# A linear-attention and GEGLU kernel: x transposed by DMA at the start, K, Q and G in 512+128 columns, a padded down projection and a bf16 Z row

## The chip, the cores and the metric

One core of a Trainium2 chip runs the whole program. The metric is the device time of one execution in microseconds (us). Nearly all executions agree within 0.3%; an execution over 1.5% above the fastest is called slow and is left out of the verdicts (in this study one of the kernel before's runs, 294.08 us, was slow; every other timed run is fast, and a kernel run only once has the state unknown). The profile is a separate recording of one execution. Its span is about 1.7 us shorter than the time of the same execution (282.7 against 284.45 before).

## The reference

```python
x = A_x                                        # 1 x 2048 x 640, bf16
g = sigmoid((x * gate_w).sum(-1, keepdims=True))
a = linear_attention(x)                        # 32 heads of 20, phi(t) = (t>0 ? t+1 : exp(t)) + 1e-6
b = (gelu(x @ w_gate) * (x @ w_up)) @ w_down   # inner width 1728
return g * a + (1 - g) * b
```

In the attention, kv = sum over s of phi(k) v, z = sum over s of phi(k), and o = phi(q) kv / (phi(q) z), then o @ wo.

## The kernel before

The kernel keeps one stream of matmuls on TensorE and hides the rest behind it. Its stages, in order:

- the head: weights and x arrive, x is transposed into xT;
- E(0): gate and up projection of the first 512 rows, in column tiles ft = 0 to 13;
- K: phi(x wk); then Q and G together, where G = x^T phi(k) replaces V;
- E(1), with the small products KV (wv^T G) and M (kv wo) in between;
- F: the output rows, 128 at a time. F(0) to F(3), E(2), F(4) to F(7), E(3), F(8) to F(15).

D(t) is a VectorE chain, which normalises row tile t of phi(q). F(t) needs it. ps tiles are the eight PSUM accumulators.

The head, on SP's queue and on TensorE:

```python
NWARM = 7                                      # dummy 128x512 matmuls on zeros
dma(out=x_sb[0][:, 0:2, :], in_=x_view[:, 0:2, :])
dma(out=wg[:, :, 0:256], in_=wg_v[:, :, 0:256])
dma(out=wu[:, :, 0:256], in_=wu_v[:, :, 0:256])
dma(out=x_sb[0][:, 2:4, :], in_=x_view[:, 2:4, :])
# ... cut ...
transpose_x(0); transpose_x(1)                 # 5 PE transposes each, copied out by ACT and DVE
# ft = 0 and 1 in halves of 256 rows: gate, gate, up, up; then transpose_x(2), (3), and again
```

The down projection. The inner width 1728 is 13.5 times 128, so the last product has only 64 rows. The two column halves hh put it in different rows of the array, next to each other:

```python
for hh in range(2):
    lo = hh * FL                               # FL = 64
    nc.tensor.matmul(accs[hh][:, 0:HALF], lhsT=hT[lo : lo + FL, NF - 1, ts],
                     rhs=wd[lo : lo + FL, NF - 1, css[hh]], start=True, stop=False)
for hh in range(2):
    # 5 matmuls with pqT and M, then 13 with hT and wd, 320 columns each; eviction: hh 0 ACT, hh 1 DVE
```

The Z row, replicated over the partitions by a product with ones in fp32:

```python
nc.tensor.matmul(zp[:, 0:HALF], lhsT=ones_f[:], rhs=zacc[:, cs], start=True, stop=True)
```

Of the kernel before, what the change touches and what calls it, by code (L numbers as in the profile page):

```python
# [16 lines left out]
def kernel(  # L17
# [21 lines left out]
    NQ = 4  # L39
# [7 lines left out]
    NWARM = 7  # L47
# [35 lines left out]
    ident = consts.tile([P, P], BF16, name="ident")  # L83
    make_identity(nc, ident[:])
    zeros_bf = consts.tile([P, QW], BF16, name="zeros_bf")
    nc.vector.memset(zeros_bf[:], 0.0)
    ones_f = consts.tile([P, P], FP32, name="ones_f")
    nc.gpsimd.memset(ones_f[:], 1.0)

    dma = nc.sync.dma_start  # L90
    dma(out=x_sb[0][:, 0:2, :], in_=x_view[:, 0:2, :])
    dma(out=wg[:, :, 0:256], in_=wg_v[:, :, 0:256])
    dma(out=wu[:, :, 0:256], in_=wu_v[:, :, 0:256])
    dma(out=x_sb[0][:, 2:4, :], in_=x_view[:, 2:4, :])
# [13 lines left out]
    for q in (1, 2, 3):  # L108
        dma(out=x_sb[q][:], in_=x_view[:, 4 * q : 4 * q + 4, :])
# [5 lines left out]
    dma(out=wd[FL:P, NF - 1, :], in_=B_w_down[FM:F, :])  # L115
# [17 lines left out]

    eneg = consts.tile([P, NT], FP32, name="eneg")
    gsc = {}

    def transpose_x(st):
        q, sl = divmod(st, 4)
        tp = psum.tile([P, 2 * QW], BF16, name="tp_x", tag="ps")
        for dk in range(ND):  # L140
            nc.tensor.transpose(
                tp[:, dk * P : (dk + 1) * P], x_sb[q][:, sl, dk * P : (dk + 1) * P], ident[:]
            )
        nc.scalar.copy(  # L144
            out=xT[q][:, 0:2, sl * P : (sl + 1) * P],
            in_=tp[:, 0 : 2 * P].rearrange("p (k n) -> p k n", k=2),
        )
        nc.vector.tensor_copy(
            out=xT[q][:, 2:5, sl * P : (sl + 1) * P],
            in_=tp[:, 2 * P : 5 * P].rearrange("p (k n) -> p k n", k=3),  # L150
        )

    hT_cur = {}
    hT0 = big.tile([P, NF, QW], BF16, name="hT0")
    hT_cur[0] = hT0
# [11 lines left out]
    def phase_E(q, ft):  # L167
# [6 lines left out]
        else:  # L174
# [4 lines left out]
            for lo in (0, FL):  # L179
                nc.vector.tensor_tensor(out=hT_cur[q][lo : lo + FL, ft, :], in0=pgu[FL:P, :],  # L180
                                        in1=gl[0:FL, :], op=ALU.mult)

    def phi(dst, src, width):
        e = work.tile([P, HALF], BF16, name="phi_e")
        nc.scalar.activation(out=e[:, :width], in_=src, func=ACT.Exp)  # L185
        m = work.tile([P, HALF], BF16, name="phi_m")
# [14 lines left out]

    def phase_K(st):
        ps0 = ps_tile("ps_k")
        proj(ps0, st, 0, HALF)
        phi(pk[st][:, 0:HALF], ps0[:, 0:HALF], HALF)
        ps1 = ps_tile("ps_k")
        proj(ps1, st, HALF, D + 1)
        phi(pk[st][:, HALF:D], ps1[:, 0:HALF], HALF)
        nc.scalar.activation(
            out=eneg[:, st : st + 1], in_=ps1[:, HALF : HALF + 1], func=ACT.Exp, scale=-1.0  # L210
        )

    def phase_Q(st, hh):
        ps = ps_tile("ps_q")
        proj(ps, st, D + 1 + hh * HALF, D + 1 + (hh + 1) * HALF)
        phi(pq[st][:, hh * HALF : (hh + 1) * HALF], ps[:, 0:HALF], HALF)

    g_sb = big.tile([P, ND, D], BF16, name="g_sb")
    g_ps = {}

    def phase_G(st, hh):
        q, sl = divmod(st, 4)
        for ct in range(ND):
            if st == 0:
                g_ps[hh, ct] = ps_tile("ps_G")
            nc.tensor.matmul(  # L226
                g_ps[hh, ct][:, 0:HALF], lhsT=x_sb[q][:, sl, ct * P : (ct + 1) * P],
                rhs=pk[st][:, hh * HALF : (hh + 1) * HALF], start=(st == 0), stop=(st == NT - 1),
            )

    def g_out(hh):
        for ct in range(ND):
            dst = g_sb[:, ct, hh * HALF : (hh + 1) * HALF]
# [8 lines left out]
    def phase_Z(st):  # L242
        if st == 0:
            return
        nc.vector.tensor_tensor(out=zacc[:], in0=(pk[0][:] if st == 1 else zacc[:]), in1=pk[st][:], op=ALU.add)
# [210 lines left out]
```

## Time and profile before

| | before |
|---|---|
| time, median of the first 5 runs | 283.5 us |
| time, median of the 15 runs up to the result | 283.94 us (283.21 to 284.61) |
| span of the profile | 282.7 us |
| TensorE busy | 97% of the span |

From the page of the kernel before: the line of busy times (engine, us, share of the span, number of instructions), and the two lines of the chain that ended last, by engine and by source line.

```profile
PE 275.6 (97%) x1708; PEld 164.2 (58%) x1721; DVE 146.1 (52%) x323; ACT 80.8 (29%) x172; POOL 2.8 (1%) x10
...
PE 95%; DMA 2%; issue 0%; SPq 0%; ACT 0%; DVE 0%; DVEq 0%
PE ps_acc L356 20%; PE ps_u L159 20%; PE ps_g L159 19%; PE ps_acc L353 8%; PE ps_q L197 8%; PE ps_k L197 8%; PE ps_G L226 8%; DMA wu<-in_B_w_up_dram 2%; PE ps_gu L159 2%; PE ps_acc L348 1%; PE ps_m L303 1%; PE ps_kv L274 1%; PE ps_z L251 0%; ACT xT L144 0%; DVE o_out L362 0%
```

TensorE is the chain from its first real work to its last. VectorE, busy for half of the span, is nearly absent from the chain. So a change gains what it takes out of the TensorE stream, plus what it takes from the two ends.

In the timeline each row has a start, a duration, an engine, a source line, the instruction with its shape and a count; the bracket is the idle time just before it and what ended it. Durations of matmuls overlap, so the cost of a group is the start of the next group minus its own start. The head of the kernel before, TensorE only:

```profile
4.75 0.74 PE L141 MATMUL tp_x<-ident,x_all 128*128 128x128 bf16 x5
5.95 1.43 PE L159 MATMUL ps_g<-xT,wg 128*128 128x256 bf16 x10 [0.46 <-ACT xT L144]
8.06 1.26 PE L159 MATMUL ps_u<-xT,wu 128*128 128x256 bf16 x10 [0.68 <-DMA wu<-in_B_w_up_dram]
9.16 0.72 PE L141 MATMUL tp_x<-ident,x_all 128*128 128x128 bf16 x10
10.34 1.25 PE L159 MATMUL ps_g<-xT,wg 128*128 128x256 bf16 x10 [0.46 <-ACT xT L144]
11.43 1.26 PE L159 MATMUL ps_u<-xT,wu 128*128 128x256 bf16 x10
12.52 0.81 PE L159 MATMUL ps_g<-xT,wg 128*128 128x512 bf16 x2
```

The last line is ft=2, where the halves of 256 rows end. Ten dense matmuls of 256 columns take 1.09 us (10.34 to 11.43); the first ten took 2.11 (5.95 to 8.06), as wu had not landed.

One row tile of F begins like this (start of F(1), timeline of TensorE):

```profile
141.80 0.57 PE L356 MATMUL ps_acc<-wd,hT 128*128 128x320 bf16 x3
142.30 0.31 PE L348 MATMUL ps_acc<-wd,hT 64*128 64x320 bf16 x2
142.54 0.85 PE L353 MATMUL ps_acc<-m_all,pqT 128*128 128x320 bf16 x5
```

Three full matmuls at the spacing of 136 ns should end 0.41 us after 141.80, but the 64-row pair starts after 0.50. The pair itself takes 0.24.

The Z product and the M block (timeline of TensorE; four passes for two fp32 products, and twelve products for M):

```profile
85.21 1.24 PE L251 MATMUL ps_z<-zacc,ones_f 128*128 128x320 f32 x4
86.29 0.84 PE L226 MATMUL ps_G<-pk,x_all 128*128 128x320 bf16 x5
...
109.99 2.21 PE L303 MATMUL ps_m<-wo_g,kvt 120*120 120x320 bf16 x12
112.14 1.04 PE L159 MATMUL ps_g<-xT,wg 128*128 128x512 bf16 x3
```

The end of the span (timeline, all engines): one eviction of 320 columns, one store.

```profile
279.32 0.55 DVE L362 TENSOR_SCALAR o_out<-ps_acc,omg_all 128x320 bf16<-128x320 f32 x1 [4.69 <-PE ps_acc L356]
279.94 0.33 SPq L365 DMA_DIRECT2D out_dram<-o_out  x1
```

### The profile page before, as it was taken

How to read it: one execution, taken by the hardware profiler on the slowest of the kernel's cores; microseconds unless marked ns; L12 is line 12 of the kernel's file. 1: busy time of each engine (PE TensorE's matmuls, PEld its weight loads, DVE VectorE, ACT ScalarE, POOL GpSimd, SP SyncE). 2: the span in 40 equal slices, each digit the busy share in tenths (PEclk: the TensorE clock that was granted, in tenths of full speed). 3: DMA queues.
4: the chain of work that ended last, by engine and by line, in shares of the span. 5: the costliest groups of instructions: out<-in, count | busy, mean ns of one | idle time of the engine just before them, and what ended most of it. 6: DMA issues, size and time to landing. Idle time of an engine off the chain costs nothing.

```text
span 282.7 us, 4315 instructions
## 1 busy us (share of the span) xinstructions
PE 275.6 (97%) x1708; PEld 164.2 (58%) x1721; DVE 146.1 (52%) x323; ACT 80.8 (29%) x172; POOL 2.8 (1%) x10
## 2 busy tenths in 40 slices
PE   7899999999999999999999999999999999999995
PEld 4644467767777765444566544456654445666663
DVE  1223369999978999999992132231113333010010
ACT  3222277753353345232200222320022222101000
POOL 3000000000000000000000000000000000000000
PEclk9999999999999999999999999999999999999999
DMA  7999999400000221332233000000100000001001
GB/s 205 330 305 186 260 361 272 150 2 0 2 1 0 49 46 27 103 83 46 50 70 96 23 0 0 2 0 23 49 23 0 2 0 0 26 23 46 26 30 40
DMA packets 35441, 20.91 MB, mean 74 GB/s; under 512 B 21214, under 2 KB 35422, under 8 KB 35422
## 3 DMA queue, kind: packets, MB, share of 16 engines
q1 hardware_dynamic: 35422, 20.65, 27.4%
q8 instruction: 13, 0.21, 0.3%
q14 instruction: 6, 0.05, 0.1%
HBM read 12.62 MB, written 2.62 MB: 54 GB/s over the span
## 4 chain that ended last, share of the span: by engine, by line
PE 95%; DMA 2%; issue 0%; SPq 0%; ACT 0%; DVE 0%; DVEq 0%
PE ps_acc L356 20%; PE ps_u L159 20%; PE ps_g L159 19%; PE ps_acc L353 8%; PE ps_q L197 8%; PE ps_k L197 8%; PE ps_G L226 8%; DMA wu<-in_B_w_up_dram 2%; PE ps_gu L159 2%; PE ps_acc L348 1%; PE ps_m L303 1%; PE ps_kv L274 1%; PE ps_z L251 0%; ACT xT L144 0%; DVE o_out L362 0%
## 5 line engine op out<-in xcount | busy, mean ns | idle before, releaser
L159 PE MATMUL ps_g<-xT,wg 128*128 128x512 bf16 (+1 forms) x257 | 64.1, 371 | 1.6 <-ACT xT L144 0.9
L159 PE MATMUL ps_u<-xT,wu 128*128 128x512 bf16 (+1 forms) x270 | 64.6, 371 | 0.7 <-DMA wu<-in_B_w_up_dram 0.7
L165 DVE TENSOR_TENSOR hT<-ps_u,gl 128x512 bf16<-128x512 f32 x52 | 35.6, 686 | 56.5 <-PE ps_u L159 56.5
L356 PE MATMUL ps_acc<-wd,hT 128*128 128x320 bf16 x416 | 61.7, 299 | 0.0
L164 ACT ACTIVATE gl<-ps_g 128x512 bf16<-128x512 f32 x52 | 30.9, 597 | 79.9 <-PE ps_g L159 76.8
L356 PEld LDWEIGHTS <-hT 128*128 128x128 bf16 x416 | 40.7, 98 | 15.8
L159 PEld LDWEIGHTS <-wu 128*128 128x128 bf16 x270 | 26.3, 98 | 30.7 <-DMA wu<-in_B_w_up_dram 1.0
L159 PEld LDWEIGHTS <-wg 128*128 128x128 bf16 x270 | 26.2, 98 | 30.2 <-issue 1.7
L362 DVE TENSOR_SCALAR o_out<-ps_acc,omg_all 128x320 bf16<-128x320 f32 x16 | 8.8, 550 | 61.6 <-PE ps_acc L356 61.6
L197 PEld LDWEIGHTS <-xT 128*128 128x128 bf16 x320 | 31.1, 97 | 12.8 <-issue 0.2
L359 ACT ACTIVATE o_out<-ps_acc,omg_all 128x320 bf16<-128x320 f32 x16 | 8.4, 527 | 68.0 <-PE ps_acc L356 68.0
L353 PE MATMUL ps_acc<-m_all,pqT 128*128 128x320 bf16 x160 | 27.1, 300 | 0.0
L197 PE MATMUL ps_q<-wqk,xT 128*128 128x320 bf16 x160 | 26.5, 299 | 0.0
L226 PE MATMUL ps_G<-pk,x_all 128*128 128x320 bf16 x160 | 26.4, 298 | 0.0
L197 PE MATMUL ps_k<-wqk,xT 128*128 128x320 bf16 (+1 forms) x160 | 22.0, 299 | 0.0
L185 ACT ACTIVATE phi_e<-ps_q 128x320 bf16<-128x320 f32 x32 | 14.0, 437 | 26.4 <-PE ps_q L197 22.7
L226 PEld LDWEIGHTS <-x_all 128*128 128x128 bf16 x160 | 15.5, 97 | 6.3 <-issue 0.2
L353 PEld LDWEIGHTS <-pqT 128*128 128x128 bf16 x160 | 14.3, 98 | 7.2
L190 DVE SCALAR_TENSOR_TENSOR pq<-ps_q,phi_m 128x320 bf16<-128x320 f32 x32 | 15.3, 480 | 0.3
L187 DVE TENSOR_SCALAR phi_m<-phi_e 128x320 bf16<-128x320 bf16 x64 | 13.8, 231 | 2.7 <-ACT phi_e L185 2.7
L185 ACT ACTIVATE phi_e<-ps_k 128x320 bf16<-128x320 f32 x32 | 13.7, 438 | 3.9 <-PE ps_k L197 3.6
L190 DVE SCALAR_TENSOR_TENSOR pk<-ps_k,phi_m 128x320 bf16<-128x320 f32 x32 | 14.4, 482 | 0.0
(52 smaller groups left out, 122.7 us busy)
## 6 DMA issues: line engine op xcount, KB each, us to landing
out_dram<-o_out SPq DMA_DIRECT2D x16, 160.0 KB, 1.8
wd<-in_B_w_down_dram SPq DMA_DIRECT2D x1, 2080.0 KB
x_all<-in_A_x_dram SPq DMA_DIRECT2D x3, 640.0 KB, 7.2
wqk<-in_A_wqkv_dram SPq DMA_DIRECT2D x2, 800.0 KB
wg<-in_B_w_gate_dram SPq DMA_DIRECT2D x1, 800.0 KB
wu<-in_B_w_up_dram SPq DMA_DIRECT2D x1, 800.0 KB
wv<-in_A_wqkv_dram SPq DMA_DIRECT2D x1, 800.0 KB
wo_g<-in_A_wo_dram SPq DMA_DIRECT2D x1, 750.0 KB, 14.7
```

What stands on the lines that cost most here:

```text
L159: nc.tensor.matmul(ps[:, t0 : t0 + tw], lhsT=w[:, dk, ft * P : (ft + 1) * P], rhs=xT[q][:, dk, t0 : t0 + tw], start=(dk == 0), stop=(dk == ...
L164: nc.scalar.activation(out=gl[:], in_=psg[:], func=ACT.Gelu_apprx_tanh)
L165: nc.vector.tensor_tensor(out=hT_cur[q][:, ft, :], in0=psu[:], in1=gl[:], op=ALU.mult)
L185: nc.scalar.activation(out=e[:, :width], in_=src, func=ACT.Exp)
L187: nc.vector.tensor_scalar(out=m[:, :width], in0=e[:, :width], scalar1=1.0, scalar2=EPS, op0=ALU.min, op1=ALU.add,)
L190: nc.vector.scalar_tensor_tensor(out=dst, in0=src, scalar=0.0, in1=m[:, :width], op0=ALU.max, op1=ALU.add,)
L197: nc.tensor.matmul(ps[:, 0 : hi - lo], lhsT=xT[q][:, dk, sl * P : (sl + 1) * P], rhs=wqk[:, dk, lo:hi], start=(dk == 0), stop=(dk == ND - 1),)
L226: nc.tensor.matmul(g_ps[hh, ct][:, 0:HALF], lhsT=x_sb[q][:, sl, ct * P : (ct + 1) * P], rhs=pk[st][:, hh * HALF : (hh + 1) * HALF], start= ...
L353: nc.tensor.matmul(acc[:, 0:HALF], lhsT=pqT[q][:, dk, ts], rhs=M["sb"][:, dk, cs], start=False, stop=False)
L356: nc.tensor.matmul(acc[:, 0:HALF], lhsT=hT[:, ft, ts], rhs=wd[:, ft, cs], start=False, stop=(ft == NF - 2))
L359: nc.scalar.activation(out=o_out[:, cs], in_=acc[:, 0:HALF], func=ACT.Copy, scale=gsc["omg"][:, st : st + 1])
L362: nc.vector.tensor_scalar(out=o_out[:, cs], in0=acc[:, 0:HALF], scalar1=gsc["omg"][:, st : st + 1], scalar2=None, op0=ALU.mult)
```

## The change

The diff, cut to its core:

```diff
-    NWARM = 7
+    NWARM = 11
-    ident = ... make_identity(...);  ones_f in FP32
+    ones_bf in BF16
-    dma(out=x_sb[0][:, 0:2, :], in_=x_view[:, 0:2, :])
-    dma(out=wg[:, :, 0:256], in_=wg_v[:, :, 0:256])
+    adma = nc.scalar.dma_start
+    nc.sync.dma_start_transpose(out=xT[0][:, :, 0:256], in_=x2[0:256, :])
+    adma(out=wg[:, :, 0:256], in_=wg_v[:, :, 0:256])
     dma(out=wu[:, :, 0:256], in_=wu_v[:, :, 0:256])
-    dma(out=x_sb[0][:, 2:4, :], in_=x_view[:, 2:4, :])
+    nc.sync.dma_start_transpose(out=xT[0][:, :, 256:512], in_=x2[256:512, :])
     # ... cut: transpose_x goes; x_sb[0] is loaded later, with the other three ...
-    dma(out=wd[FL:P, NF - 1, :], in_=B_w_down[FM:F, :])
+    nc.gpsimd.memset(wd[FL:P, NF - 1, :], 0.0)      # and the same rows of hT0 and hT1
-            for lo in (0, FL):                      # hT's last tile written twice
-                nc.vector.tensor_tensor(out=hT_cur[q][lo : lo + FL, ft, :], ...)
+            nc.vector.tensor_tensor(out=hT_cur[q][0:FL, ft, :], ...)
+    CH = ((0, QW), (QW, D))                         # 512 + 128 columns for K, Q and G
+    # G: one accumulator at a time over all 16 row tiles, a share of it after each Q(st);
+    #    before: five accumulators at once, in two sweeps over st
-            nc.tensor.matmul(zp[:, 0:HALF], lhsT=ones_f[:], rhs=zacc[:, cs], ...)
+            nc.tensor.matmul(zp[:, 0:HALF], lhsT=ones_bf[:], rhs=zsum[:, cs], ...)
-    phase_E(1, 1); phase_M()                        # M in one block
+    for ft in range(2, NF):
+        phase_E(1, ft)
+        if 0 <= ft - 3 < NG: phase_M(ft - 3)
+        phase_D(ft - 1)
     # phase_F
-        # pair of 64-row matmuls first, then 5 + 13 per half
+        # 5 + 14 full matmuls per half; the fourteenth is padded with zeros
+            if last and hh == 1:
+                na = 144                            # ACT evicts 144 columns, DVE 176
+            if last:
+                dma(out=out2[st * P : (st + 1) * P, cs], in_=o_out[:, cs])
```

Z, too, moves: before, the fp32 product stood early in the second sweep of Q and G (85 us); after, it stands near the end of Q and G.

More of the change, by code (lines that the diff above doesn't have):

```diff
@@ L6 @@
 from concourse._compat import with_exitstack
-from concourse.masks import make_identity
 ACT = mybir.ActivationFunctionType
@@ L81 @@
     pq = [big.tile([P, D], BF16, name=f"pq{t}") for t in range(NT)]
-    ident = consts.tile([P, P], BF16, name="ident")
-    make_identity(nc, ident[:])
     zeros_bf = consts.tile([P, QW], BF16, name="zeros_bf")
     nc.vector.memset(zeros_bf[:], 0.0)
-    ones_f = consts.tile([P, P], FP32, name="ones_f")
-    nc.gpsimd.memset(ones_f[:], 1.0)
+    ones_bf = consts.tile([P, P], BF16, name="ones_bf")
+    nc.gpsimd.memset(ones_bf[:], 1.0)
     dma = nc.sync.dma_start
-    dma(out=x_sb[0][:, 0:2, :], in_=x_view[:, 0:2, :])
-    dma(out=wg[:, :, 0:256], in_=wg_v[:, :, 0:256])
+    adma = nc.scalar.dma_start
+    nc.sync.dma_start_transpose(out=xT[0][:, :, 0:256], in_=x2[0:256, :])
+    adma(out=wg[:, :, 0:256], in_=wg_v[:, :, 0:256])
     dma(out=wu[:, :, 0:256], in_=wu_v[:, :, 0:256])
-    dma(out=x_sb[0][:, 2:4, :], in_=x_view[:, 2:4, :])
+    nc.sync.dma_start_transpose(out=xT[0][:, :, 256:512], in_=x2[256:512, :])
     warm = consts.tile([P, 1], FP32, name="act_warm")
@@ L107 @@
     dma(out=wqk[:, :, D + 1 : WQK], in_=wqkv_v[:, :, 0:D])
-    for q in (1, 2, 3):
+    for q in range(NQ):
         dma(out=x_sb[q][:], in_=x_view[:, 4 * q : 4 * q + 4, :])
@@ L132 @@
     )
+    nc.gpsimd.memset(wd[FL:P, NF - 1, :], 0.0)
     eneg = consts.tile([P, NT], FP32, name="eneg")
     gsc = {}
-    def transpose_x(st):
-        q, sl = divmod(st, 4)
-        tp = psum.tile([P, 2 * QW], BF16, name="tp_x", tag="ps")
-        for dk in range(ND):
-            nc.tensor.transpose(
-                tp[:, dk * P : (dk + 1) * P], x_sb[q][:, sl, dk * P : (dk + 1) * P], ident[:]
-            )
-        nc.scalar.copy(
-            out=xT[q][:, 0:2, sl * P : (sl + 1) * P],
-            in_=tp[:, 0 : 2 * P].rearrange("p (k n) -> p k n", k=2),
-        )
-        nc.vector.tensor_copy(
-            out=xT[q][:, 2:5, sl * P : (sl + 1) * P],
-            in_=tp[:, 2 * P : 5 * P].rearrange("p (k n) -> p k n", k=3),
-        )
     hT_cur = {}
     hT0 = big.tile([P, NF, QW], BF16, name="hT0")
+    nc.gpsimd.memset(hT0[FL:P, NF - 1, :], 0.0)
     hT_cur[0] = hT0
@@ L178, in phase_E @@
             nc.scalar.activation(out=gl[0:FL, :], in_=pgu[0:FL, :], func=ACT.Gelu_apprx_tanh)
-            for lo in (0, FL):
-                nc.vector.tensor_tensor(out=hT_cur[q][lo : lo + FL, ft, :], in0=pgu[FL:P, :],
-                                        in1=gl[0:FL, :], op=ALU.mult)
+            nc.vector.tensor_tensor(out=hT_cur[q][0:FL, ft, :], in0=pgu[FL:P, :],
+                                    in1=gl[0:FL, :], op=ALU.mult)
     def phi(dst, src, width):
-        e = work.tile([P, HALF], BF16, name="phi_e")
+        e = work.tile([P, QW], BF16, name="phi_e")
         nc.scalar.activation(out=e[:, :width], in_=src, func=ACT.Exp)
-        m = work.tile([P, HALF], BF16, name="phi_m")
+        m = work.tile([P, QW], BF16, name="phi_m")
         nc.vector.tensor_scalar(
@@ L200, in proj @@
             )
+    CH = ((0, QW), (QW, D))
     def phase_K(st):
-        ps0 = ps_tile("ps_k")
-        proj(ps0, st, 0, HALF)
-        phi(pk[st][:, 0:HALF], ps0[:, 0:HALF], HALF)
-        ps1 = ps_tile("ps_k")
-        proj(ps1, st, HALF, D + 1)
-        phi(pk[st][:, HALF:D], ps1[:, 0:HALF], HALF)
+        for lo, hi in CH:
+            ps = ps_tile("ps_k")
+            proj(ps, st, lo, hi + (hi == D))
+            phi(pk[st][:, lo:hi], ps[:, 0 : hi - lo], hi - lo)
         nc.scalar.activation(
-            out=eneg[:, st : st + 1], in_=ps1[:, HALF : HALF + 1], func=ACT.Exp, scale=-1.0
+            out=eneg[:, st : st + 1], in_=ps[:, D - QW : D - QW + 1], func=ACT.Exp, scale=-1.0
@@ L211, in phase_K @@
         )
-    def phase_Q(st, hh):
-        ps = ps_tile("ps_q")
-        proj(ps, st, D + 1 + hh * HALF, D + 1 + (hh + 1) * HALF)
-        phi(pq[st][:, hh * HALF : (hh + 1) * HALF], ps[:, 0:HALF], HALF)
-    g_sb = big.tile([P, ND, D], BF16, name="g_sb")
-    g_ps = {}
-    def phase_G(st, hh):
-        q, sl = divmod(st, 4)
-        for ct in range(ND):
-            if st == 0:
-                g_ps[hh, ct] = ps_tile("ps_G")
-            nc.tensor.matmul(
-                g_ps[hh, ct][:, 0:HALF], lhsT=x_sb[q][:, sl, ct * P : (ct + 1) * P],
-                rhs=pk[st][:, hh * HALF : (hh + 1) * HALF], start=(st == 0), stop=(st == NT - 1),
-            )
@@ L231, in g_out, with phase_Q @@
-    def g_out(hh):
-        for ct in range(ND):
-            dst = g_sb[:, ct, hh * HALF : (hh + 1) * HALF]
-            if ct % 2 == 0:
-                nc.vector.tensor_copy(out=dst, in_=g_ps[hh, ct][:, 0:HALF])
-            else:
-                nc.scalar.copy(out=dst, in_=g_ps[hh, ct][:, 0:HALF])
+    def phase_Q(st):
+        for lo, hi in CH:
+            ps = ps_tile("ps_q")
+            proj(ps, st, D + 1 + lo, D + 1 + hi)
+            phi(pq[st][:, lo:hi], ps[:, 0 : hi - lo], hi - lo)
@@ new lines, with g_units @@
+    g_sb = big.tile([P, ND, D], BF16, name="g_sb")
+    def g_units():
+        for lo, hi in CH:
+            for ct in range(ND):
+                gp = ps_tile("ps_G")
+                for st in range(NT):
+                    nc.tensor.matmul(
+                        gp[:, 0 : hi - lo], lhsT=x_all[:, st, ct * P : (ct + 1) * P],
+                        rhs=pk[st][:, lo:hi], start=(st == 0), stop=(st == NT - 1),
+                    )
+                    if st < NT - 1:
+                        yield hi - lo
+                nc.scalar.copy(out=g_sb[:, ct, lo:hi], in_=gp[:, 0 : hi - lo])
+                yield hi - lo
@@ L239 @@
     zacc = consts.tile([P, D], FP32, name="zacc")
+    zsum = consts.tile([P, D], BF16, name="zsum")
     zrep = consts.tile([P, D], FP32, name="zrep")
@@ L244, in phase_Z @@
             return
-        nc.vector.tensor_tensor(out=zacc[:], in0=(pk[0][:] if st == 1 else zacc[:]), in1=pk[st][:], op=ALU.add)
+        nc.vector.tensor_tensor(out=(zsum[:] if st == NT - 1 else zacc[:]), in0=(pk[0][:] if st == 1 else zacc[:]),
+                                in1=pk[st][:], op=ALU.add)
     def phase_Zrep():
@@ L250, in phase_Zrep @@
             cs = slice(hh * HALF, (hh + 1) * HALF)
-            nc.tensor.matmul(zp[:, 0:HALF], lhsT=ones_f[:], rhs=zacc[:, cs], start=True, stop=True)
+            nc.tensor.matmul(zp[:, 0:HALF], lhsT=ones_bf[:], rhs=zsum[:, cs], start=True, stop=True)
             nc.scalar.copy(out=zrep[:, cs], in_=zp[:, 0:HALF])
@@ L292, with phase_M @@
     M = {}
-    def phase_M():
-        m_all = ov.tile([P, ND + NG, D], BF16, name="m_all", tag="slab_c")
-        m_sb = m_all[:, 0:ND, :]
-        m_st = m_all[:, ND : ND + NG, :]
-        M["sb"] = m_sb
-        for g in range(NG):
-            for hh in range(2):
-                cs = slice(hh * HALF, (hh + 1) * HALF)
-                mp = ps_tile("ps_m")
-                nc.tensor.matmul(mp[0 : gw[g], 0:HALF], lhsT=kvt[0 : gw[g], g, 0 : gw[g]],
-                                 rhs=wo_g[0 : gw[g], g, cs], start=True, stop=True)
-                if hh == 0:
-                    nc.vector.tensor_copy(out=m_st[0 : gw[g], g, cs], in_=mp[0 : gw[g], 0:HALF])
-                else:
-                    nc.scalar.copy(out=m_st[0 : gw[g], g, cs], in_=mp[0 : gw[g], 0:HALF])
-            lo = GW * g
-            hi = lo + gw[g]
-            while lo < hi:
-                k = lo // P
-                e = min(hi, (k + 1) * P)
-                dma(out=m_sb[lo - k * P : e - k * P, k, :], in_=m_st[lo - GW * g : e - GW * g, g, :])
-                lo = e
+    def phase_M(g):
+        if g == 0:
+            M["all"] = ov.tile([P, ND + NG, D], BF16, name="m_all", tag="slab_c")
+        m_sb = M["all"][:, 0:ND, :]
+        m_st = M["all"][:, ND : ND + NG, :]
+        for hh in range(2):
+            cs = slice(hh * HALF, (hh + 1) * HALF)
+            mp = ps_tile("ps_m")
+            nc.tensor.matmul(mp[0 : gw[g], 0:HALF], lhsT=kvt[0 : gw[g], g, 0 : gw[g]],
+                             rhs=wo_g[0 : gw[g], g, cs], start=True, stop=True)
+            if hh == 0:
+                nc.vector.tensor_copy(out=m_st[0 : gw[g], g, cs], in_=mp[0 : gw[g], 0:HALF])
+            else:
+                nc.scalar.copy(out=m_st[0 : gw[g], g, cs], in_=mp[0 : gw[g], 0:HALF])
+        lo = GW * g
+        hi = lo + gw[g]
+        while lo < hi:
+            k = lo // P
+            e = min(hi, (k + 1) * P)
+            dma(out=m_sb[lo - k * P : e - k * P, k, :], in_=m_st[lo - GW * g : e - GW * g, g, :])
+            lo = e
     pqT = {}
@@ L342, in phase_F @@
         ts = slice(sl * P, (sl + 1) * P)
-        o_out = work.tile([P, D], BF16, name="o_out", bufs=3)
-        accs = [ps_tile("ps_acc") for _ in range(2)]
-        css = [slice(hh * HALF, (hh + 1) * HALF) for hh in range(2)]
+        o_out = work.tile([P, D], BF16, name="o_out", bufs=2)
+        last = st == NT - 1
         for hh in range(2):
-            lo = hh * FL
-            nc.tensor.matmul(accs[hh][:, 0:HALF], lhsT=hT[lo : lo + FL, NF - 1, ts],
-                             rhs=wd[lo : lo + FL, NF - 1, css[hh]], start=True, stop=False)
@@ L350, in phase_F @@
-        for hh in range(2):
-            acc, cs = accs[hh], css[hh]
+            acc = ps_tile("ps_acc")
+            cs = slice(hh * HALF, (hh + 1) * HALF)
             for dk in range(ND):
                 nc.tensor.matmul(acc[:, 0:HALF], lhsT=pqT[q][:, dk, ts],
-                                 rhs=M["sb"][:, dk, cs], start=False, stop=False)
-            for ft in range(NF - 1):
+                                 rhs=M["all"][:, dk, cs], start=(dk == 0), stop=False)
+            for ft in range(NF):
@@ L356, in phase_F @@
                 nc.tensor.matmul(acc[:, 0:HALF], lhsT=hT[:, ft, ts],
-                                 rhs=wd[:, ft, cs], start=False, stop=(ft == NF - 2))
-            if hh == 0:
-                nc.scalar.activation(out=o_out[:, cs], in_=acc[:, 0:HALF], func=ACT.Copy,
-                                     scale=gsc["omg"][:, st : st + 1])
-            else:
-                nc.vector.tensor_scalar(out=o_out[:, cs], in0=acc[:, 0:HALF],
-                                        scalar1=gsc["omg"][:, st : st + 1], scalar2=None,
-                                        op0=ALU.mult)
@@ L365, in phase_F @@
-        dma(out=out2[st * P : (st + 1) * P, :], in_=o_out[:])
-    transpose_x(0)
-    transpose_x(1)
-    e01 = [(ps_tile("ps_g"), ps_tile("ps_u")) for _ in range(2)]
-    for hb in range(2):
-        if hb == 1:
-            transpose_x(2)
-            transpose_x(3)
-        for ft in range(2):
-            e_mm(e01[ft][0], wg, ft, 0, hb * 256, 256)
-        for ft in range(2):
-            e_mm(e01[ft][1], wu, ft, 0, hb * 256, 256)
-    for ft in range(2):
+                                 rhs=wd[:, ft, cs], start=False, stop=(ft == NF - 1))
@@ new lines, in phase_F @@
+            omg = gsc["omg"][:, st : st + 1]
+            na = HALF if hh == 0 else 0
+            if last and hh == 1:
+                na = 144
+            if na:
+                nc.scalar.activation(out=o_out[:, hh * HALF : hh * HALF + na], in_=acc[:, 0:na],
+                                     func=ACT.Copy, scale=omg)
+            if na < HALF:
+                nc.vector.tensor_scalar(out=o_out[:, hh * HALF + na : (hh + 1) * HALF], in0=acc[:, na:HALF],
+                                        scalar1=omg, scalar2=None, op0=ALU.mult)
@@ new lines, in phase_F @@
+            if last:
+                dma(out=out2[st * P : (st + 1) * P, cs], in_=o_out[:, cs])
+        if not last:
+            dma(out=out2[st * P : (st + 1) * P, :], in_=o_out[:])
+    e01 = [(ps_tile("ps_g"), ps_tile("ps_u")) for _ in range(2)]
+    for ft in range(2):
+        e_mm(e01[ft][0], wg, ft, 0, 0, 256)
+    e_mm(e01[0][1], wu, 0, 0, 0, 256)
+    e_mm(e01[1][1], wu, 1, 0, 0, 256)
+    for ft in range(2):
+        e_mm(e01[ft][0], wg, ft, 0, 256, 256)
+        e_mm(e01[ft][1], wu, ft, 0, 256, 256)
@@ L385 @@
     phase_gate()
+    gu = g_units()
+    done = 0
+    total = NT * ND * D
     for st in range(NT):
-        phase_Q(st, 0)
-        phase_G(st, 0)
+        phase_Q(st)
         phase_Z(st)
-    LAG = 3
-    for st in range(NT + LAG):
-        if st < NT:
-            phase_Q(st, 1)
-        if st == 1:
-            g_out(0)
-        if st == LAG + 1:
-            phase_Zrep()
-        if st == LAG + 2:
-            phase_KV(0, 2)
-        if st >= LAG:
-            phase_G(st - LAG, 1)
-    g_out(1)
+        while done < total * (st + 1) // (NT + 1):
+            done += next(gu)
+    phase_Zrep()
+    for w in gu:
+        pass
+    phase_KV(0, 4)
     hT_cur[1] = ov.tile([P, NF, QW], BF16, name="hT1", tag="slab_b")
+    nc.gpsimd.memset(hT_cur[1][FL:P, NF - 1, :], 0.0)
+    phase_E(1, 0)
+    phase_KV(4, NG)
+    phase_E(1, 1)
     phase_D(0)
-    phase_E(1, 0)
-    phase_KV(2, NG)
-    phase_E(1, 1)
-    phase_M()
     for ft in range(2, NF):
         phase_E(1, ft)
-        if ft - 1 < NT:
-            phase_D(ft - 1)
+        if 0 <= ft - 3 < NG:
+            phase_M(ft - 3)
+        phase_D(ft - 1)
     for st in range(NF - 1, NT):
```

## The prediction

> **What bounds the kernel now.** TensorE. The page gives PE 97% of a 282.7 us span; the chain of waits is 95% PE, 2% DMA. The clock row is at full speed from about 5.5 us on. Start to start in the timeline, dense matmuls are spaced 215.8 ns at 512 columns, 135.8 at 320, about 55.7 at 120 to 128 (ps_kv, the transposes), each with its own weight load. This agrees with the Trainium skill, "TensorE: Matmul & The Clock Gate", section "Wait — 56ns, not 53.3ns?": N/2.4 + 2.5 ns. Only fewer streamed columns, fewer PE gaps, a shorter head or tail can gain.
>
> **Costs, stage by stage (chain effect).**
>
> 1. Head. The first gate matmul starts at 5.95 us and ft=2 at 12.52; in between are 40 matmuls of 256 columns (109 ns each, 4.36 us dense), ten transposes (0.56) and about 1.65 us of waits (0.96 for wu, 0.68 for the xT copies). After: no transposes or copies; eleven warm matmuls (nine or ten at 427 ns cold) end near 5.75. Later transposes of 512 rows took 3.3 us of issue each, so I estimate 1.7 us for 256 rows: wu is issued near 2.7 instead of 1.8, the second transpose near 3.1, x now arrives in 256 B packets (about 290 KB/us at best in the trace, against 360 for 1280 B). I expect waits for wu or the second transpose of 0.5 to 1 us and ft=2 at about 11.0: **-1.5 us** (0.3 to 2.3).
>
> 2. 512+128 instead of 320+320 columns: 5 x (215.8+56) = 1359 ns against 2 x 5 x 135.8 = 1358 per row tile. **0 us**.
>
> 3. Z replication in bf16 instead of fp32: four passes of 268 ns become two of 136: **-0.8 us**.
>
> 4. Down projection: the paired 64-row matmuls start 3 ns apart, then take 240, and the matmul before them is stretched by 96 ns (232 against 136). That is 339 ns per row tile, against 2 x 136 = 272 for two zero-padded full ones: 67 ns x 16 = **-1.1 us**.
>
> 5. M and KV gaps (283, 227, 172 instead of 136 ns in ps_m) go when M is spread over E(1): **-0.3 us**.
>
> 6. Tail: last eviction 0.55 us becomes about 0.35, split over two engines, and the last store is halved: **-0.3 us**.
>
> 7. New risk: zrep now comes after nearly all of Q and G (about 101 us instead of 87), so all sixteen normalisations (2.6 us of VectorE each) run from there. My VectorE sum in the new order (41.6 + 8.5 hT + 3.4 others) frees the first accumulator of F about 1 us before E(2,0) needs it,, not 11. A stall of 0 to 2 us is possible: **+0.2 us**.
>
> **Sum:** about -3.9; predicted 279.5 us, range 278.0 to 281.4. Chances: faster by over 2% 0.10, within 2% 0.88, slower 0.02.
>
> **What would show it.** ft=2 starting at 10.5 to 11.7 us; ps_k, ps_q, ps_G spaced 216 and 56 with no new idle; ps_z 136; each row tile of F 5.16 us instead of 5.24, without the 232 ns step; VectorE near full from 101 to about 153 us; PE still about 97%.
>
> **What would make it wrong.** The first transposes landing late (DMA start-up, or 256 B packets colliding with the weights), moving waits to ft=2; 128-column matmuls not hiding weight loads; the VectorE backlog stalling PE in E(1) or at E(2,0); G waiting for pk at its first unit.

## The result

The kernel after takes 279.59 us (median of 8 runs, 279.49 to 280.28), against 283.94. The ratio is 0.9849, 95% interval 0.9836 to 0.9861. A ratio is the mean time of one kernel's fast runs over that of the other's of the same rounds, so it is not quite the ratio of the medians. The gain of 1.5% is clear of noise.

From the page of the kernel after, the same parts:

```profile
PE 271.9 (98%) x1682; PEld 155.6 (56%) x1703; DVE 138.5 (50%) x309; ACT 79.4 (29%) x175; POOL 4.1 (1%) x11
...
PE 96%; DMA 2%; issue 0%; DVE 0%; ACT 0%
```

The head (timeline of TensorE):

```profile
5.68 1.25 PE L142 MATMUL ps_g<-xT,wg 128*128 128x256 bf16 x10 [0.18 <-DMA xT<-in_A_x_dram]
6.92 1.26 PE L142 MATMUL ps_u<-xT,wu 128*128 128x256 bf16 x10
8.03 0.71 PE L142 MATMUL ps_g<-xT,wg 128*128 128x256 bf16 x5
...
10.42 1.03 PE L142 MATMUL ps_g<-xT,wg 128*128 128x512 bf16 x4
```

The first gate matmul starts on the landing of the transposed x, 0.27 us earlier than before; from there the stream is almost dense (wu holds it up by about 0.15 us ahead of 6.92). One of the five records of the first gate group of ft=2 is missing (x4), so that group began 0.216 us before the 10.42 shown, at 10.21.

The start of a row tile of F, the Z product with the 128-column G matmuls behind it, and the end of the span:

```profile
138.15 0.57 PE L331 MATMUL ps_acc<-wd,hT 128*128 128x320 bf16 x3
138.56 0.84 PE L328 MATMUL ps_acc<-m_all,pqT 128*128 128x320 bf16 x5
...
99.15 0.43 PE L231 MATMUL ps_z<-zsum,ones_bf 128*128 128x320 bf16 x2
99.42 1.45 PE L208 MATMUL ps_G<-pk,x_all 128*128 128x128 bf16 x23
100.70 1.26 PE L254 MATMUL ps_kv<-g_sb,wv 128*120 128x120 bf16 x20
...
274.46 0.38 ACT L338 ACTIVATE o_out<-ps_acc,omg_all 128x144 bf16<-128x144 f32 x1 [2.00 <-PE ps_acc L331]
274.88 0.40 DVE L341 TENSOR_SCALAR o_out<-ps_acc,omg_all 128x176 bf16<-128x176 f32 x1 [4.97 <-ACT o_out L338]
275.30 0.33 SPq L344 DMA_DIRECT2D out_dram<-o_out  x1
```

No step stands in front of ps_acc now (138.15 to 138.56 is 3 x 136 ns). Z takes 0.27 us instead of 1.08. The 23 G matmuls of 128 columns take 1.28 us, 55.7 ns each, though each loads its own weights. And at the end the two pieces of the split eviction do not overlap: VectorE waited for ScalarE.

The next table gives the length of each stage, worked out from the starts of its first matmul and of the next stage's first matmul in the two traces.

| stage | before, us | after, us | difference |
|---|---|---|---|
| head, to ft=2 | 12.52 | 10.21 | -2.31 |
| rest of E(0) | 24.82 | 24.82 | 0 |
| K | 21.86 | 21.85 | -0.01 |
| Q, G, Z, first part of KV | 45.32 | 44.92 | -0.40 |
| E(1), rest of KV, M | 32.54 | 31.60 | -0.94 |
| F(0) to F(3) | 20.86 | 20.65 | -0.21 |
| E(2), E(3) together | 58.46 | 58.28 | -0.18 |
| F(4) to F(7) | 20.86 | 20.65 | -0.21 |
| F(8) to the start of the last matmul | 41.68 | 41.16 | -0.52 |
| from there to the end | 3.82 | 3.73 | -0.09 |

Ten KV matmuls of 55 ns moved from E(1) to the stage ahead of it, so 0.55 us belongs to the fourth row rather than the fifth: they gained 0.95 and 0.39. All rows but the head sum to -2.56. The two profiles differ by 4.9 us, the median times by 4.35; the experiments show why.

### The profile page after: what moved, and what is told of

The parts are those of the page before. It is cut to its first block, busy times and chain, and to the rows that moved or that the text cites. A ratio compares the mean times of both kernels' runs of the same rounds, so it can differ in the third digit from the quotient of the medians.

```text
span 277.9 us, 4292 instructions
## 1 busy us (share of the span) xinstructions
PE 271.9 (98%) x1682; PEld 155.6 (56%) x1703; DVE 138.5 (50%) x309; ACT 79.4 (29%) x175; POOL 4.1 (1%) x11
## 4 chain that ended last, share of the span: by engine, by line
PE 96%; DMA 2%; issue 0%; DVE 0%; ACT 0%
PE ps_acc L331 22%; PE ps_u L142 20%; PE ps_g L142 20%; PE ps_q L179 8%; PE ps_acc L328 8%; PE ps_k L179 8%; PE ps_G L208 8%; DMA xT<-in_A_x_dram 2%; PE ps_gu L142 2%; PE ps_m L282 1%; PE ps_kv L254 1%; DVE o_out L341 0%; ACT o_out L338 0%; PE ps_z L231 0%
## 5 line engine op out<-in xcount | busy, mean ns | idle before, releaser
L341 DVE TENSOR_SCALAR o_out<-ps_acc,omg_all 128x320 bf16<-128x320 f32 (+1 forms) x16 | 8.5, 535 | 57.1 <-PE ps_acc L331 49.3
L338 ACT ACTIVATE o_out<-ps_acc,omg_all 128x320 bf16<-128x320 f32 (+1 forms) x17 | 8.7, 518 | 73.8 <-PE ps_acc L331 59.1
L179 PE MATMUL ps_q<-wqk,xT 128*128 128x128 bf16 (+1 forms) x157 | 24.3, 297 | 0.2
L208 PE MATMUL ps_G<-pk,x_all 128*128 128x128 bf16 (+1 forms) x158 | 24.1, 298 | 0.1
L179 PE MATMUL ps_k<-wqk,xT 128*128 128x129 bf16 (+1 forms) x157 | 21.9, 298 | 0.2
L169 DVE TENSOR_SCALAR phi_m<-phi_e 128x512 bf16<-128x512 bf16 x64 | 12.6, 235 | 14.5 <-ACT phi_e L167 14.4
L167 ACT ACTIVATE phi_e<-ps_q 128x512 bf16<-128x512 f32 (+1 forms) x32 | 12.4, 435 | 21.6 <-PE ps_q L179 19.7
L167 ACT ACTIVATE phi_e<-ps_k 128x512 bf16<-128x512 f32 (+1 forms) x32 | 12.8, 439 | 5.8 <-PE ps_k L179 5.0
L172 DVE SCALAR_TENSOR_TENSOR pk<-ps_k,phi_m 128x512 bf16<-128x512 f32 (+1 forms) x32 | 14.2, 481 | 0.2
L172 DVE SCALAR_TENSOR_TENSOR pq<-ps_q,phi_m 128x512 bf16<-128x512 f32 (+1 forms) x32 | 14.2, 483 | 0.0
```

Of the source, the lines that this page charges most:

```text
L167: nc.scalar.activation(out=e[:, :width], in_=src, func=ACT.Exp)
L169: nc.vector.tensor_scalar(out=m[:, :width], in0=e[:, :width], scalar1=1.0, scalar2=EPS, op0=ALU.min, op1=ALU.add,)
L172: nc.vector.scalar_tensor_tensor(out=dst, in0=src, scalar=0.0, in1=m[:, :width], op0=ALU.max, op1=ALU.add,)
L179: nc.tensor.matmul(ps[:, 0 : hi - lo], lhsT=xT[q][:, dk, sl * P : (sl + 1) * P], rhs=wqk[:, dk, lo:hi], start=(dk == 0), stop=(dk == ND - 1),)
L208: nc.tensor.matmul(gp[:, 0 : hi - lo], lhsT=x_all[:, st, ct * P : (ct + 1) * P], rhs=pk[st][:, lo:hi], start=(st == 0), stop=(st == NT - 1),)
L338: nc.scalar.activation(out=o_out[:, hh * HALF : hh * HALF + na], in_=acc[:, 0:na], func=ACT.Copy, scale=omg)
```

## The experiments

Eleven kernels were run; all gave correct results. "Against after" compares with the kernel after, which was timed in another round (the three rounds of experiments ran on different chips, and the kernel before had medians of 283.86, 284.35 and 283.9 us in them), so the two ratios to the kernel before are the fair comparison and differences of medians are given beside them. Across the eleven traces every stage that an edit does not touch is equal to 0.03 us (the end to 0.07), with one exception: the head, which differs from run to run (experiment 1 shows with what). So stages are compared in the traces, and the head also by times.

### 1. The head alone

The kernel before with the head's part of the diff (transposes by DMA, eleven warm matmuls, wg on ACT's queue) and nothing else.

> The kernel before with the head of the kernel after and nothing else: x of the first 512 rows by two DMA transposes, eleven warm matmuls, the first wg load on ACT's queue. Theory 1 (the head is a stage of its own, and its gain passes whole to the end): ft=2 starts at 10.2 us as in the kernel after, against 12.5, nothing later gives it back, span 280.4, so -2.0 to -2.4 us. Rival (part of the 2.3 us is owed to the later order, for instance to the POOL memsets or to a lighter DMA stream, or is eaten at the K stage where x_all and wqk arrive later): less than -1.5 us.

Measured: 282.27 us against 283.86, ratio 0.9944 (0.9926 to 0.9962), so about -1.6 us. In its trace ft=2 starts at 10.07, and every later stage has the length of the kernel before. So the gain passes whole to the end, as theory 1 says. Its size was missed: -1.6 is less than -2.0 to -2.4, and by the times alone the rival (less than 1.5) would stay open; it falls by the stages of the trace. Yet the trace says -2.5 against the profile of before. The reason is in the heads of the other runs:

| trace | first gate matmul | ft=2 |
|---|---|---|
| PE transposes: before | 5.95 | 12.52 |
| PE transposes: pad_only | 5.96 | 12.15 |
| DMA transposes: eight kernels with the head of after | 5.56 to 6.06 | 10.07 to 10.96, mean 10.41 |

In the eight heads with DMA transposes the spread goes with the moment at which the clock record of the trace turns to full. It turned at 4.46, 4.66, 4.74, 5.18, 6.13, 6.23, 6.85 and 7.20 us, and ft=2 started at 10.07, 10.07, 10.21, 10.35, 10.40, 10.45, 10.75 and 10.96, in the same order. Where it turns late, the first gate matmuls run at 213 ns instead of 109. This is the latest of the eight (after_320), whose first ten take 1.63 us instead of 1.09:

```profile
6.06 1.79 PE L142 MATMUL ps_g<-xT,wg 128*128 128x256 bf16 x10
7.69 1.25 PE L142 MATMUL ps_u<-xT,wu 128*128 128x256 bf16 x10
```

With PE transposes the two heads differ by the landing of wu instead: the first up matmul starts at 8.06 in the kernel before and at 7.69 in pad_only.

The profiled execution of the kernel before was one with a long head (its time was 284.45, above the median of 283.94). The medians differ by 4.35, of which the later stages are 2.56, which leaves 1.8 for the head. The directly timed head_only gave 1.6, with an interval from 1.1 to 2.1.

### 2. Only the queue of wg, in the kernel before

```diff
-    dma(out=wg[:, :, 0:256], in_=wg_v[:, :, 0:256])
+    nc.scalar.dma_start(out=wg[:, :, 0:256], in_=wg_v[:, :, 0:256])
```

> The kernel before with only its first wg load moved to ACT's queue; PE transposes stay. Theory 1 (the wait for wu before was competition among loads issued within 3 us, and PE transposes plus copies stood in line): wg and x land a little earlier, wu still lands at 7.5 to 8.0, ft=2 at 12.0 to 12.5, time -0.0 to -0.5 us. Rival (the second queue alone is what brings wu early): wu lands near 6.9 and ft=2 near 11.2, -1.2 us or more.

Measured: 283.54 us, ratio 0.9988 (0.9971 to 1.0006); ft=2 at 11.61, the first up matmul at 7.16. The interval reaches from -0.8 us to +0.2, so the size is not settled. The rival's -1.2 us lies outside it: the second queue alone is not what the new head gains. In the trace, though, theory 1 missed both of its marks (wu at 7.5 to 8.0, ft=2 at 12.0 to 12.5): the up matmul at 7.16 follows the gate matmuls with no wait for wu.

### 3. wg on SP's queue, in the kernel after

```diff
-    adma = nc.scalar.dma_start
+    adma = nc.sync.dma_start
```

> The kernel after with its first wg load on SP's queue behind the first transpose. Theory 1 (the head is bound by the bytes and by the first transpose, not by who issues them): wg issued near 2.2, wu near 2.7; the first transpose lands earlier than 5.66, wg near 6, ft=2 at 10.2 to 10.8, time 0 to +0.5 us against the kernel after. Rival (the second queue carries the gain): ft=2 at 11.2 or later, +1 us or more.

Measured: 280.36 us, ratio to before 0.9878 (0.9856 to 0.9899), about +0.8 us against after, though the two intervals overlap slightly. Its trace (SP's queue and TensorE):

```profile
0.81 1.34 SPq L89 DMA_TRANSPOSE xT<-in_A_x_dram  x1
...
2.21 0.56 SPq L90 DMA_DIRECT2D wg<-in_B_w_gate_dram  x1
...
6.47 1.26 PE L142 MATMUL ps_g<-xT,wg 128*128 128x256 bf16 x10 [0.69 <-DMA wg<-in_B_w_gate_dram]
```

SP is busy issuing the transpose for 1.3 us, so wg is issued at 2.21 instead of 0.81. Now the first gate matmul waits for wg, not for x, and starts at 6.47, outside the range of 5.56 to 6.06 of the other eight. Theory 1 was too small (0 to +0.5, ft=2 by 10.8), the rival's trace mark (ft=2 at 11.2 or later) was not reached either: ft=2 started at 10.88. The Trainium skill says in "DMA: Bandwidth & Descriptors", section "Rules for kernel authors", that issuing from several engines only saves the sequencer's issue time. That agrees with this trace, and here the issue time of a transpose stands in front of a load that the chain waits for.

### 4. Seven warm matmuls, in the kernel after

```diff
-    NWARM = 11
+    NWARM = 7
```

> The kernel after with seven warm matmuls instead of eleven. PE then idles from 4.2 us to the landing of the first transpose near 5.66. Theory 1 (the first gate matmul is bound by that landing; the extra warm matmuls only keep the clock): it starts at 5.7 as before, but part of the first matmuls may run at the cold 213 ns, ft=2 at 10.2 to 11.3. Rival (PE is bound by the warm matmuls themselves): the first gate matmul starts earlier than 5.5.

Measured: 281.21 us, ratio to before 0.9908 (0.9889 to 0.9927), +1.6 us against after.

```profile
1.26 3.17 PE L116 MATMUL warm_ps<-zeros_bf 128*128 128x512 bf16 x7 [1.26 <-DVE zeros_bf L83]
5.51 2.29 PE L142 MATMUL ps_g<-xT,wg 128*128 128x256 bf16 x10 [1.08 <-DMA xT<-in_A_x_dram]
7.59 2.15 PE L142 MATMUL ps_u<-xT,wu 128*128 128x256 bf16 x10
9.57 0.71 PE L142 MATMUL ps_g<-xT,wg 128*128 128x256 bf16 x5
```

Here the first gate matmul is bound by the landing of x, as theory 1 says. (With eleven warm matmuls that is not always so. In three of the eight heads, after_dve_plus, after_tail_small and after_z32_mblock, the clock was still slow, the eleventh warm matmul started at 5.50, and the first gate matmul followed 427 ns behind it at 5.93; in the first two of them x had landed at 5.59 and 5.45. There the rival holds.) But the first twenty matmuls take 208 and 198 ns each on average (5.51 to 7.59 to 9.57) instead of 109: TensorE ran at the slow clock until 9.4 us, and ft=2 started at 11.76, later than the 10.2 to 11.3 expected. So the four extra warm matmuls are not decoration. Without them the loss is 1.35 us against the mean head of after. The ratio to before says more: -2.6 us (-2.1 to -3.1), of which the later stages are 2.56. So with seven warm matmuls the new head gains nothing that the times can show. What eleven would do in the kernel before was not run. The Trainium skill, "TensorE: Matmul & The Clock Gate", section "Part 1: The HAM clock gate (the "warmup" mystery)", says that the slow clock is the default and that about 3.4 us of activity in a free-running window releases it. The traces agree: with eleven warm matmuls, from 1.26 us on, the clock record turns to full between 4.46 and 7.20 us after the span's start, varying by run; with a hole of about 1.3 us after the seventh it turned at 9.41 (one trace).

### 5. The padding alone, in the kernel before

```diff
-            lo = hh * FL
-            nc.tensor.matmul(accs[hh][:, 0:HALF], lhsT=hT[lo : lo + FL, NF - 1, ts],
-                             rhs=wd[lo : lo + FL, NF - 1, css[hh]], start=True, stop=False)
+            nc.tensor.matmul(accs[hh][:, 0:HALF], lhsT=hT[:, NF - 1, ts],
+                             rhs=wd[:, NF - 1, css[hh]], start=True, stop=False)
```

With it go the zeroed rows and the single write of hT's last tile, as in the change.

> The kernel before with only the paired 64-row matmuls of the down projection replaced by two zero-padded 128-row ones in the same place. Theory 1 (a change of the active rows between matmuls exposes a weight load of some 96 ns before and 103 ns after the pair): each row tile of F takes 5.16 us instead of 5.24, no step of 232 or 240 ns is left, -1.1 to -1.25 us in all. Rival (the 96 and 103 ns belong to the start of a new accumulator or to its semaphore waits): the steps stay with the padded matmuls and the time grows by 16 x 136 ns, +1 to +2 us.

Measured: 283.03 us against 284.35, ratio 0.9957 (0.9941 to 0.9973), -1.2 us. In the trace the stages E(1) to F(15) gain 0.09 + 0.21 + 0.09 + 0.21 + 0.09 + 0.52 = 1.21 us.

```profile
140.83 1.11 PE L355 MATMUL ps_acc<-wd,hT 128*128 128x320 bf16 x7
141.78 0.43 PE L347 MATMUL ps_acc<-wd,hT 128*128 128x320 bf16 x2
142.05 0.84 PE L352 MATMUL ps_acc<-m_all,pqT 128*128 128x320 bf16 x5
```

Seven full matmuls take 0.95 us and the padded two 0.27, all at 136 ns. The new accumulators start in the same place as before, so their start did not cost the step. The rival falls.

### 6. 64 rows, neither paired nor padded, in the kernel after

```diff
             for ft in range(NF):
-                nc.tensor.matmul(acc[:, 0:HALF], lhsT=hT[:, ft, ts], rhs=wd[:, ft, cs], ...)
+                pr = P if ft < NF - 1 else FL
+                nc.tensor.matmul(acc[:, 0:HALF], lhsT=hT[0:pr, ft, ts], rhs=wd[0:pr, ft, cs], ...)
```

> The kernel after with the fourteenth matmul of each half on its 64 real rows only, unpaired and not padded, at the end of the half; fewer products for the same streamed columns. Theory 1 (change of active rows): each of the 32 costs about 96 ns before and 103 ns after it more than a full one, spacing 232 before and 239 after, +6.4 us (+5.5 to +6.8) against the kernel after. Rival (the cost belongs to the accumulator start): 0 us, spacing 136.

Measured: 286.02 us in a single run (state unknown), +6.4 us; in the trace F(0) to F(3) takes 22.31 us instead of 20.65 and F(8) onward 44.39 instead of 41.16, about 0.2 us per 64-row matmul.

```profile
135.81 0.31 PE L332 MATMUL ps_acc<-wd,hT 64*128 64x320 bf16 x1
136.05 0.85 PE L328 MATMUL ps_acc<-m_all,pqT 128*128 128x320 bf16 x5
136.74 2.17 PE L332 MATMUL ps_acc<-wd,hT 128*128 128x320 bf16 x14
```

The matmul of 64 rows takes 0.24 us instead of 0.136, and again there is a step of 96 ns ahead of it. Both move with the matmul to the end of the half, where no accumulator starts. A matmul on half of the rows costs more here than one on all of them.

The kernel after has the same step in two other places, where nothing was edited. The last pair of M uses 40 rows and 40 columns of the array instead of 120: it starts 309 ns after the matmul ahead of it instead of 216, and the matmul behind it 229 ns later instead of 136 (122.99, 123.30, 123.45 and 123.68 us). The last KV matmuls keep 128 rows but use 40 columns instead of 120, and they too start 93 ns late (148 ns instead of 55, at 104.32). So the step is not special to 64 rows, nor to rows.

### 7. 320+320 columns, in the kernel after

```diff
-    CH = ((0, QW), (QW, D))
+    CH = ((0, HALF), (HALF, D))
```

> The kernel after with 320+320 columns instead of 512+128 in K, Q and G, all else equal. Theory 1 (128-column matmuls hide their weight loads, so both splits stream at N/2.4 + 2.5 ns): 0 us, within 0.3, against the kernel after; spacing 136. Rival (the wide split saves stalls of PSUM or weight loads): +0.5 us or more.

Measured: 279.44 us, ratio to before 0.9838 (0.982 to 0.9856); against after 0 within the intervals. K takes 21.86 us and the stage of Q and G 44.91, against 21.85 and 44.92. The split is neutral, as expected. (Its profiled execution was a longer one, 280.32, with ft=2 at 10.96.)

### 8. Z in fp32 and M in one block, in the kernel after

```diff
-                nc.tensor.matmul(zp[:, 0:HALF], lhsT=ones_bf[:], rhs=zsum[:, cs], ...)
+                nc.tensor.matmul(zp[:, 0:HALF], lhsT=ones_f[:], rhs=zacc[:, cs], ...)
-        if 0 <= ft - 3 < NG: phase_M(ft - 3)
+    for g in range(NG): phase_M(g)     # after E(1,1)
```

> The kernel after with the Z replication in fp32 again and with M in one block after E(1,1). Theory 1: ps_z is spaced 268 ns in four passes (+0.8 us) and the M block shows gaps of 90 to 190 ns again (+0.3 us): +1.1 us (0.8 to 1.5) against the kernel after, visible in those two places of the trace. Rival (these gains are hidden behind other waits): under +0.4 us.

Measured: 280.53 us, ratio to before 0.9868 (0.985 to 0.9886). In the trace the stage with Z is 45.77 us instead of 44.92 (+0.85) and E(1) 31.77 instead of 31.60 (+0.17), so +1.02 together, inside the expected range. The medians differ by 0.94. In this experiment M is worth about half of what was expected of it, because its block has gaps of only 0.39 us in all, where the kernel before has 0.51; 0.20 of this stays in the kernel after, mostly as the steps around the 40-row pair of experiment 6.

### 9. The last eviction in one piece, in the kernel after

```diff
-                na = 144
+                na = 0
```

> The kernel after with the last eviction whole on VectorE (320 columns) instead of split 144 on ScalarE and 176 on VectorE; the store stays halved. The trace of the kernel after shows the two pieces one after the other (274.46 to 274.84, then 274.88 to 275.28). Theory 1 (the split is serial, so it costs instead of saving): last eviction done about 0.55 us after it starts instead of 0.82, -0.2 to -0.3 us against the kernel after. Rival (the split saves): +0.1 us or more.

Measured: 279.67 us, ratio to before 0.9849 (0.9836 to 0.9863), so no difference that times can show; but the run-to-run spread of the head is larger than the effect. In the trace, where the end is measured by itself, it is 3.51 us from the last matmul's start to the end of the span, instead of 3.73.

```profile
274.66 0.55 DVE L341 TENSOR_SCALAR o_out<-ps_acc,omg_all 128x320 bf16<-128x320 f32 x1 [4.61 <-PE ps_acc L331]
275.24 0.33 SPq L344 DMA_DIRECT2D out_dram<-o_out  x1
```

One piece of 0.55 us beats two pieces in a row (0.82 from 274.46 to 275.28). The split costs 0.22 us; the halved store is what made the end shorter. In the built kernel the VectorE piece has a semaphore wait for ScalarE's, and a build (not run) that gave the two pieces separate output tiles still had that wait. So the order comes from the program as built. What is left in common is the accumulator. The Trainium skill, "PSUM — Partial Sum Buffer", section "Terms", says that two engines at once at the same bank and quadrant (32 partitions) are an error, reads against reads included. That would explain why they are put in order, but no run here shows such an error.

### 10. The last row tile in 512+128 columns

```diff
-        for hh in range(2):                               # 320 + 320 in every tile
+        for hh, (c0, c1) in enumerate(CH if last else ((0, HALF), (HALF, D))):
```

with ScalarE evicting the first piece, VectorE the second, and one store for each in the last tile.

> The kernel after with its last row tile in 512 and 128 columns instead of two of 320, the 512 evicted by ScalarE while PE works on the last 128, the 128 by VectorE in one piece of about 0.28 us; the same streamed columns. Theory 1: from the last matmul to the end of the span 3.1 to 3.3 us instead of 3.73; -0.4 to -0.6 us against the kernel after, the best kernel here. Rival (the end is bound by the fixed landing of the last store alone): 0 to -0.2 us.

Measured: 279.35 us (5 runs, 279.19 to 279.76), ratio to before 0.984 (0.9827 to 0.9854).

```profile
273.69 0.69 ACT L336 ACTIVATE o_out<-ps_acc,omg_all 128x512 bf16<-128x512 f32 x1 [6.15 <-PE ps_acc L332]
273.72 0.94 PE L332 MATMUL ps_acc<-wd,hT 128*128 128x128 bf16 x14
274.40 1.07 SPq L341 DMA_DIRECT2D out_dram<-o_out  x2
274.76 0.35 DVE L338 TENSOR_SCALAR o_out<-ps_acc,omg_all 128x128 bf16<-128x128 f32 x1 [4.61 <-PE ps_acc L332]
```

The wide piece is evicted and its store issued while TensorE works on the narrow one. From the last matmul's start to the end it takes 3.09 us instead of 3.73; 0.08 of this is only the shorter last matmul (128 columns instead of 320), so 0.56 us is gained. This is the lowest median. Against the kernel after, the medians differ by 0.24 us, less than the expected 0.4 to 0.6 (the head of the profiled execution was 0.24 us longer than in the kernel after), and the intervals overlap (and after_320 has 279.44), so its lead is shown by the trace of the end, not by the times.

### 11. Useless work on VectorE, in the kernel after

```diff
+        for _ in range(2 if st < 8 else 1):
             nc.vector.tensor_tensor(out=prod[:], in0=pq[st][:], in1=zrep[:], op=ALU.mult)
```

> The kernel after with the product pq x zrep computed twice in the first eight normalisations, 8 x 0.74 = 5.9 us of useless VectorE work. In the trace of the kernel after the first VectorE eviction of F ends at 152.5 and PE needs that accumulator at 155.1: 2.6 us to spare. Theory 1 (the late start of the normalisations cost nothing because of this slack, and only just): PE stalls about 3.3 us (2.5 to 4) near E(2,0), and the time grows by that. Rival (VectorE is far off the chain): under +0.5 us.

Measured: 281.41 us in a single run (state unknown). In the trace one stage grew, E(2), from 29.14 to 30.26 us: +1.12 us, less than the expected 2.5 to 4. In the kernel after, the first VectorE eviction of F and TensorE's E(2):

```profile
151.93 0.55 DVE L341 TENSOR_SCALAR o_out<-ps_acc,omg_all 128x320 bf16<-128x320 f32 x1
...
155.12 1.24 PE L142 MATMUL ps_u<-xT,wu 128*128 128x512 bf16 x5
...
157.28 1.24 PE L142 MATMUL ps_u<-xT,wu 128*128 128x512 bf16 x5
```

and with the added work:

```profile
158.35 0.55 DVE L342 TENSOR_SCALAR o_out<-ps_acc,omg_all 128x320 bf16<-128x320 f32 x1
...
155.67 1.24 PE L142 MATMUL ps_u<-xT,wu 128*128 128x512 bf16 x5
...
158.96 1.24 PE L142 MATMUL ps_u<-xT,wu 128*128 128x512 bf16 x5 [0.96 <-DVE o_out L342]
```

The eviction came 6.4 us later on this clock, of which 0.54 is the longer head. The matmul that waited for it is the up matmul of ft=1, two accumulators later than I had counted. The expectation took the accumulators to be reused strictly eight tiles apart; in the built kernel they are not. With the right matmul the slack in the kernel after is 157.28 - 152.48 = 4.8 us, and 5.9 - 4.8 = 1.1, which is what was measured. So both readings are half right: VectorE is off the chain in the kernel after, but only by 4.8 us at this place.

## Why the prediction was right, point by point

The predicted 279.5 us and range held (279.59), and "within 2%" was the likeliest class. That the time was met within 0.1 us is partly luck. The gain was 4.35 us and not 3.9 (the terms as listed add up to 3.8), and the prediction started from about 283.4, near the first median of 283.5, while the median of all 15 runs is 283.94; the two errors cancel. The terms of the sum:

| term | predicted | measured |
|---|---|---|
| head | -1.5 (0.3 to 2.3 less) | -1.6 timed alone (-1.1 to -2.1), -1.8 from the medians, -2.3 between the two profiles |
| 512+128 columns | 0 | 0 (after_320) |
| Z in bf16 | -0.8 | -0.80 between the two traces, -0.85 in the experiment |
| down projection | -1.1 | -1.21 |
| M and KV gaps | -0.3 | -0.31 between the two traces, all of it M; -0.17 for M in the experiment |
| tail | -0.3 | -0.09 |
| VectorE backlog | +0.2 | 0 |
| two gaps among the first G matmuls | not foreseen | -0.16 |

The two middle stages gained 0.95 + 0.39 = 1.34. Start to start, the two traces show where: Z 0.80 (four passes of 268 ns to two of 136), M 0.31 (its gaps fell from 0.51 to 0.20), the padding's part in E(1) 0.09, and 0.16 for two gaps of the kernel before (0.03 at 60.42 and 0.13 ahead of 62.08), where a G group goes over to Q, which are absent in the new order. The gaps at KV are the same in both kernels.

- The head. The mechanism held in part: the copies, the transposes and most of the wait for wu are gone. The new head has less waiting than the 0.5 to 1 us that I allowed for, 0.17 us in its trace; wu held up the up matmul at 6.92 by only 0.15 although it was issued later (2.21 instead of 1.81). But points that I had treated as details carry the gain as much: the warm matmuls (1.6 us when four are left out, as much as the whole gain) and the second queue (about 0.8 us, with overlapping intervals).
- The down projection. Right in size and mechanism: two experiments move the 96 and 103 ns with the 64-row matmul and with nothing else. That these are weight loads that can't be hidden is argued from their size (one load takes 98 ns in the profile), not shown. In the trace the load of the 64-row matmul starts 4 ns ahead of its matmul, while in the dense stream a load starts about 135 ns ahead. That fits a late load, but also an array that must first run empty when the shape of its active part changes; no run here tells the two apart.
- The tail is the term that was mis-sized. The step that failed is "last eviction 0.55 us becomes about 0.35, split over two engines". The split ran in series and took 0.82. The halved store, which I had counted as the smaller part, saved about 0.3.
- The backlog. VectorE was busy without a gap of more than 0.04 us from 100.3 to 153.8 us, as predicted (101 to about 153), and no stall came of it. The "about 1 us" of slack was wrong: it is 4.8 us, because I assumed the wrong matmul to be the one that waits.
- The other feared causes (late weights at ft=2, 128-column matmuls exposing weight loads, G waiting for pk) do not show in the trace.

## What to carry to other kernels

Cost matmuls by start-to-start spacing in the trace, not by rows used: a half-height matmul in a full-height stream cost about 0.1 us on each side, so two padded ones (272 ns) were cheaper than a packed pair (about 340 ns). The length of a head varies from run to run, here with the moment at which the clock turned to full and with the landing of a weight, and a single profile can mis-size it by half a microsecond; time that part alone. Keep TensorE busy right up to the first landing, as a hole of 1.3 us cost 1.6, but not much beyond it (the eleventh warm matmul, when still slow, ended 0.3 to 0.5 us after x had landed). At the end of a kernel, evict from two accumulators rather than split one between engines, and make the last piece small.

## What the Trainium skill lacked or had wrong

- "TensorE: Matmul & The Clock Gate", section "The mechanism": the packing of small matmuls is described by the few ns between starts, and the trace has that too for the pair of 64 rows (3 ns). It lacks the cost of going between full-height and half-height matmuls: 96 ns before and 103 ns after, with a single matmul as with a pair (0.24 instead of 0.136 us, plus the step ahead), and 93 ns at a change to 40 rows or 40 columns. "TensorEngine Tiling (Array Packing)" has a drain of TensorE at a change of tiling mode, but no time for it.
- The same page, section "The mechanism", says that weight loads overlap with running matmuls only when the row group differs (a sentence further up in the section also allows loads into a background buffer). Here loads of full-height weights were hidden behind full-height matmuls of the same rows: 23 G matmuls of 128 columns, each with its own load, took 55.7 ns each, and the extra time came where the rows changed.
- The same page, section "Back-to-back issue gap", gives about 131 ns at 512 columns and 81 ns at 128 for streams of load and matmul pairs. These streams ran at 215.8 and 55.7 ns, which is the formula for isolated matmuls on that page (N/2.4 + 2.5). At 120 columns the formula gives 52.5 ns; the KV matmuls ran at 55.0.
- "DMA: Bandwidth & Descriptors" gives the issue of a DMA transpose on the generations before trn3 B0 only as cycle counts (from HBM for small tiles, and for 8,192 tiles within SBUF), not for one from HBM of this size: 256 rows of 640 took 1.35 us of SP's queue and landed 4.83 us after its issue began, with other loads in flight.
- "PSUM — Partial Sum Buffer" names the bank rule, but not its cost for an eviction split between two engines: 0.82 us in two pieces against 0.55 in one.
